# Paired products in the attention's first and last steps, a re-ordered first stage and an earlier first v load in an adaLN transformer block

## The chip, the cores and the metric

The kernel runs on one core of a Trainium2 chip. The metric is device time in microseconds (us) of one execution, as the median of several runs. The core has five engines that run their own instruction queues: TensorE (PE in the profile; its weight loads are PEld), VectorE (DVE), ScalarE (ACT), GpSimd (POOL) and SyncE (SP), which here issues the DMA transfers.

## The reference

One sequence of S = 2048 rows with D = 512 columns passes through an attention block of 32 heads (16 columns each) and a token-mixing MLP; both are modulated by six vectors that come from a condition `c`.

```python
mod = (silu(c) @ w_mod).reshape(1, 6, 1, 512)          # sa, ca, ga, sb, cb, gb
h = layernorm(x) * (1 + ca) + sa
q, k, v = split(h @ wqkv)                               # 32 heads of 16
o = softmax(q @ k.T * 16 ** -0.5) @ v
x = x + ga * (o @ wo)
h = layernorm(x) * (1 + cb) + sb
# B: token mixing by shifted columns, then an MLP 512 -> 1792 -> 512
t = gelu(layernorm(h) @ w1);  t = concat(four quarters of t, shifted by +1, -1, +2, -2 rows)
h1 = h + t @ w2
x = x + gb * (h1 + gelu(layernorm(h1) @ w3) @ w4)
```

All arithmetic is to float32 precision. The kernel gets it from split operands: a float32 matrix is held as a high part (rounded) and a low part (the rest), and a product is three matmuls (high by high, high by low, low by high).

## The kernel before, in words

**The work.** Rows come in four chunks of 512 (`NC`, index `ci`), four tiles of 128 rows each. Heads come in 16 pairs. An attention unit is one chunk of queries with one pair of heads: 64 units, each of 16 key tiles, so 1024 steps (`NS`), index `s`. A unit needs, before its exponentials, the row maximum of its scores. So each step has two parts: the score part of step `s`, and the maximum part of step `s + LEAD` with LEAD = 24.

- `score_part` (L1028): for head `j` of the pair, a matmul of 64 contraction rows with 512 columns (L1042) into a PSUM bank, then an exponential by ScalarE (L1038). The result is held as a 32-bit pattern whose upper half is the high part of the probability.
- `p_low` (L1078): the lower half becomes a float16 by a halving (L1093), on GpSimd for both heads at once, or on ScalarE in two halves (L1088) when the plan has GpSimd behind; the second ScalarE half waits in the list `second`.
- `pv_part` (L1100): probabilities by v, for the high parts (L1119) and the low parts of two steps (L1116), summed over a unit in one bank.
- `max_part` (L1010): another 64-row matmul (L1026) into a bank, and VectorE's `reduce_max` over it (L1022). When a unit's maxima are complete, `max_fin` (L1059) puts their negatives into rows of the query tile by eight small DMAs.

**Pairs.** Head 0 uses contraction rows 0 to 63 and head 1 rows 64 to 127. `row_pair(s, j)` (L1044) puts the score product of head `j` and the maximum product of head `1 - j` next to each other, on the two halves of the array. A counter `x` walks over 2 x 1024 such rows plus 48 ahead: `s, i = divmod(x, 2)`. For `s < 0` (24 steps) there are only maxima, for the last 24 steps only scores; there a row holds one product.

**The first stage** (to about 63 us in the profile). `x` is loaded by chunk. `ln1` (L536) takes statistics on VectorE (L372, L373), the reciprocal root on GpSimd (L376, L377), and normalizes each tile on VectorE (`apply`, L550) or ScalarE (`apply_act`, L553, the tiles in `LNA[ci]`). `mod_cols` (L567) computes sa and ca as rows (L572), copies them out of PSUM (L578, L580), turns them into columns by eight products with a 1x1 tile `one` (L587), and copies them to `modcol` (L591). `ln1_T` (L608) transposes each chunk in four slices of 128 columns (L618) and modulates them: for slices in `LNV[ci]` ScalarE makes the high part from PSUM (L627) and VectorE the whole (L630), for others ScalarE makes the whole (L623) and then the high part (L644); the low part is a subtraction (L636) on GpSimd for slices in `LNG[ci]`, else on VectorE. `qk_first` (L647) computes the first group's k for each chunk and q for chunk 0, 12 matmuls each (L361, L363, L365), and `qk_store` sends them to DRAM, from where `load_first` (L935) fetches the operands of the first unit. `v_weights` (L800) bounds |v| (L812 to L831), scales and splits v's weights. `v_tiles` (L754) computes v per 128 rows; `store` (L776) writes a tile to DRAM (`Vs`) and, once the attention's tiles exist (`direct`), also straight to its place in `vst`. The tiles stored before that are fetched from `Vs` by `before(s)` (L1590) at `s = -1` (the first entry of `VAT`, L1603).

**The order of work.** The order on every engine is written by a planner when the kernel is built: `Sched` keeps a clock per engine (P, A, D, G, and S for SP) and adds planned costs in nanoseconds. A `chain` is a sequence of operations on A, D and G with planned costs, a priority `prio` (lower goes first when an engine is behind) and a time at which it is ready. Generators (`mod_cols`, `ln1_T`, `qk_first`, the qkv groups, the tails) are the fillers on TensorE: each `yield` is one matmul's cost or a condition that must hold before it goes on. The main loop (L1666 to L1732) chooses at each point between a row, a block of pv columns (`do_cols`) and fillers. `one` is the planned time at which enough of the seven shared PSUM banks (`NSM`) are free; `need` (L1682) is how many products the row has. A row is entered when the time to it is under `STAY` (within a burst of up to `GRP` = 3 rows) or `BACK` (a new burst), where the next engine in need may be let run dry only to within `EARLY`; fillers may run past that time by `GRACE`. `budget(s)` spreads the fillers over the steps. `Sched.dma` plans SP: at least 475 ns per transfer.

**The last stage.** The tail of chunk `ci` (L1256: wo, LayerNorms, shifts, MLP) is filler during the attention of the next chunk; that of the last chunk runs after the attention.

Of the kernel before, what the change touches and what calls it, by code (L numbers as in the profile page):

```python
# [41 lines left out]
LAG = 2  # L42
CARRY = 3000.0
# [7 lines left out]
OVER = 3000.0  # L51
# [26 lines left out]
LNA = ((2, 3),) * 4  # L78
LNG = ((0, 1, 2),) * 4
LNV = ((1, 3),) * 4  # L80
# [11 lines left out]
GRACE = 400.0  # L92
PTLOW = 3
OVER = 1500.0

class Sched:
# [23 lines left out]
    def dma(self, start, o, i):  # L120

        n = 2 if o.dtype == BF16 else 4
        for d in o.shape:
            n *= d
        start(o, i)  # L125
        self.T["S"] = max(self.T["S"], self.T["P"]) + max(n / DBW, 475.0)
        return self.T["S"] + DLAT
# [205 lines left out]
def kernel(ctx, tc, A_x, A_wqkv, A_wo, B_w1, B_w2, B_w3, B_w4, c, w_mod, out):  # L333
# [57 lines left out]
    one = con.tile([1, 1], F32, name="one")  # L391
    pool.memset(one, 1.0)
# [143 lines left out]
    def ln1(ci):  # L536
        x = xt[ci]
        st, mv, rs = [sp.tile([P, TPC, n], F32, name=f"{nm}{ci}") for nm, n in (("st", 6), ("mv", 2), ("rs", 2))]
        left = [TPC]

        def stats(t):
            ln_stats(st[:, t, :], mv[:, t, :], x[:, t, :])

        def rstd():
            rstd_of(rs[:, :, 0], mv[:, :, 1])
            pool.tensor_tensor(rs[:, :, 1], mv[:, :, 0], rs[:, :, 0], op=OP.mult)
            pool.tensor_tensor(rs[:, :, 1], rs[:, :, 1], mone, op=OP.mult)

        def apply(t):
            dve.tensor_scalar(x[:, t, :], x[:, t, :], mv[:, t, 0:1], rs[:, t, 0:1], op0=OP.subtract, op1=OP.mult)  # L550

        def apply_act(t):
            act.activation(x[:, t, :], x[:, t, :], AF.Identity, bias=rs[:, t, 1:2], scale=rs[:, t, 0:1])  # L553
# [12 lines left out]

    def mod_cols():  # L567
# [18 lines left out]
        for i in range(8):  # L586
            te.matmul(b[:, i:i + 1], row[:, i * P:(i + 1) * P], one, start=True, stop=True, skip_group_check=True)  # L587
# [5 lines left out]
        sch.chain(("D", 120, cols), mark(("mod", 0)), mark(("mod", 1)), prio=0, bank=b)  # L593
# [14 lines left out]
    def ln1_T():  # L608
        yield lambda: ("mod", 0) in done and ("mod", 1) in done
        for ci in range(NC):  # L610
            x = xt[ci]
            left = [KT]
            for k in range(KT):
# [3 lines left out]
                for t in range(TPC):  # L617
                    te.transpose(b[:, t * P:(t + 1) * P], x[:, t, k * P:(k + 1) * P], ident)  # L618
                    yield 110
# [19 lines left out]
                def one(left=left, ci=ci):  # L639
# [3 lines left out]
                ops = (("A", 660, high), ("D", cD(), whole)) if k in LNV[ci] else (  # L643
                    ("A", 660, modulate), ("A", cA(), lambda f=f, hi=hi: act.activation(hi, f, AF.Copy)))  # L644
                sch.chain(*ops, (e, cG() if e == "G" else cD(), low), (None, 0, one))
# [154 lines left out]
    def v_weights(a):  # L800
# [4 lines left out]
        for i in range(2):  # L805
# [6 lines left out]
            sch.chain(("D", 1200, lambda x=f.bitcast(F32), t=t: dve.scalar_tensor_tensor(  # L812
# [13 lines left out]
        def cols():  # L826
            for i in range(2):
                dve.tensor_tensor_reduce(out=scr, in0=vb[:, i * P:(i + 1) * P], in1=ident, scale=1.0, scalar=0.0,
                                         op0=OP.mult, op1=OP.add, accum_out=vcol[:, 2 * a + i:2 * a + i + 1])
            dve.tensor_scalar(vcol[:, 2 * a:2 * a + 2], vcol[:, 2 * a:2 * a + 2], VHI, None, op0=OP.mult)  # L830
            dve.reciprocal(vb, vb)  # L831
            qfree.extend(ts)

        def scaled():
            for i, (f, f3) in enumerate(st):
                c = slice(512 * i, 512 * i + 512)
                sch.chain(("G", cG(), lambda f3=f3: pool.tensor_tensor(f3, f3, vb[:, None, :].to_broadcast([P, 2, 256]),
# [3 lines left out]
        sch.chain(("D", cD(256), bound), ("D", 1000, cols), (None, 0, scaled), bank=b)  # L841
# [202 lines left out]
    def row_pair(s, j):  # L1044

        parts = []
        if 0 <= s < NS:
            parts.append((j, score_part(s, j)))
        if s + LEAD < NS:
            parts.append((1 - j, max_part(s + LEAD, 1 - j)))  # L1050
        parts = [x for _, x in sorted(parts, key=lambda x: x[0])]
# [5 lines left out]
        return [partial(x[2], e) for x in parts]  # L1057
# [532 lines left out]
    def before(s):  # L1590
# [4 lines left out]
        if asked:  # L1595
# [23 lines left out]
    def one_row(x):  # L1619
# [3 lines left out]
        if second:  # L1623
            second.pop(0)()
# [22 lines left out]
    def do_cols(n):  # L1647
        sch.to("c")
# [17 lines left out]
    while x < end or pvs or acs:  # L1666
# [109 lines left out]
```

## Time and profile before

| | |
|---|---|
| median of 3 runs | 1995.44 us (1993.75 to 1995.77) |
| the profiled execution | 1993.19 us |
| its span, first to last instruction | 1991.4 us |
| mean granted TensorE clock | 0.991 |
| TensorE, VectorE, ScalarE, GpSimd busy | 1933.8, 1669.9, 1483.2, 1671.0 us |
| first maximum product (L1026) starts | 63.3 us |
| first score product (L1042) starts | 97.5 us |
| last maximum product | 1791.2 us |
| last score product | 1821.8 us |
| products of maxima, of scores | 2048, 2048 |

The views of the profile: the page with busy times, the chain of work that ended last and the costliest groups; windows (busy time of each engine in a stretch); groups by line; timelines (instructions in order of time, merged, with the idle time ahead of them and what ended it in brackets); and waits (engine and line that waited, for whom, total us, times, longest). Times are microseconds from the span's start, means of groups nanoseconds. Matmuls are pipelined: a matmul's duration is longer than the distance to the next one, so the price of a matmul is read from starts.

### The profile page before, as it was taken

The numbers are of one execution on the slowest core, as the hardware profiler recorded it, in microseconds if no ns is written. First come the engines' busy times: TensorE is split into PE (matmuls) and PEld (weight loads), VectorE is DVE, ScalarE is ACT, GpSimd is POOL, SyncE is SP. The second block draws the span as 40 slices with busy tenths as digits, with TensorE's granted clock in tenths as the row PEclk, the third lists the DMA queues.
The fourth block names the chain that finished last, engine by engine and source line by source line (L and its number), as shares of the span: only waits on it lengthen the run. The fifth ranks groups of instructions, "written<-read, shape, count | busy, mean of one in ns | idle before, by whom it ended". The sixth has DMA issues, their size and how long they took to land.

```text
span 1991.4 us, 42269 instructions
## 1 busy us (share of the span) xinstructions
PE 1933.8 (97%) x14480; PEld 1137.1 (57%) x14480; DVE 1669.9 (84%) x3010; ACT 1483.2 (74%) x3081; POOL 1671.0 (84%) x1601
## 2 busy tenths in 40 slices
PE   6989999999999999999999999999999999999899
PEld 4654565555445555555455555555555555555798
DVE  6969878899999888998999988888998888892643
ACT  5366888788878777787888877787888777786443
POOL 5368999999999998998898999888898988897532
PEclk8999999999999999999999999999999999999999
DMA  5675788786533433434433333344433334433432
GB/s 180 193 209 177 217 254 249 252 271 206 163 103 115 136 109 112 145 127 132 133 114 111 108 112 101 110 140 132 157 115 103 96 112 136 132 100 108 186 143 91
DMA packets 233082, 293.23 MB, mean 147 GB/s; under 512 B 125876, under 2 KB 178052, under 8 KB 216580
## 3 DMA queue, kind: packets, MB, share of 16 engines
q1 hardware_dynamic: 232868, 290.53, 45.8%
q8 instruction: 115, 1.88, 0.4%
q14 instruction: 99, 0.81, 0.1%
HBM read 225.81 MB, written 62.91 MB: 145 GB/s over the span
## 4 chain that ended last, share of the span: by engine, by line
PE 69%; DVE 9%; POOL 6%; ACT 6%; DMA 2%; issue 2%; SPq 1%; POOLq 0%; ACTq 0%; DVEq 0%
PE mb L1026 14%; PE sc L1042 11%; PE pv L1119 10%; PE w L361 7%; PE w L363 7%; PE w L365 7%; PE pv L1116 6%; DVE mx L1022 6%; POOL pt L1093 4%; ACT pt L1038 3%; PE ot L1151 1%; SPq L125 1%; DMA wr<-Ws 1%; PE q L365 1%; PE q L361 1%
## 5 line engine op out<-in xcount | busy, mean ns | idle before, releaser
L1022 DVE TENSOR_REDUCE mx<-mb 128x1 f32<-128x512 f32 x2048 | 1283.7, 682 | 117.2 <-PE mb L1026 88.6
L1093 POOL TENSOR_SCALAR pt<-pt 128x1024 f16<-128x1024 uint16 x980 | 1301.2, 1369 | 82.1 <-ACT pt L1038 78.6
L1038 ACT ACTIVATE pt<-sc 128x512 int32<-128x512 f32 x2048 | 1102.1, 602 | 272.5 <-PE mb L1026 181.2
L1026 PE MATMUL mb<-kst,qtl 64*128 64x512 f32 x2048 | 754.0, 455 | 18.3 <-DVE mx L1022 7.0
L1042 PE MATMUL sc<-qtl,kst 64*128 64x512 f32 x2048 | 728.3, 445 | 1.6 <-ACT pt L1038 0.7
L1026 PEld LDWEIGHTS mb<-kst,qtl 64*128 64x128 f32 x2048 | 347.1, 192 | 228.6 <-DVE mx L1022 108.4
L1042 PEld LDWEIGHTS sc<-qtl,kst 64*128 64x128 f32 x2048 | 334.9, 185 | 155.9 <-issue 52.5
L1119 PE MATMUL pv<-pt,vst 128*32 128x512 f16 x4096 | 348.8, 392 | 5.5 <-DMA vst<-Vs 4.9
L1116 PE MATMUL pv<-pt,vst 128*17 128x512 f16 (+1 forms) x2048 | 215.7, 397 | 4.6 <-POOL pt L1093 4.3
L1453 POOL TENSOR_TENSOR g<-xs,g 128x256 fp32r<-128x256 f32 (+2 forms) x144 | 103.4, 719 | 92.7 <-ACT g L1452 88.7
L1119 PEld LDWEIGHTS <-vst 128*32 128x32 bf16 x4096 | 112.3, 94 | 112.3 <-issue 48.1
L361 PE MATMUL w<-A,wr 128*128 128x256 f32 (+2 forms) x576 | 172.0, 299 | 0.6 <-ACT A L355 0.3
L363 PE MATMUL w<-A,wr 128*128 128x256 f32 (+2 forms) x576 | 170.0, 295 | 0.5 <-DVE A L351 0.3
L365 PE MATMUL w<-A,wr 128*128 128x256 f32 (+2 forms) x576 | 169.2, 294 | 0.0
L1116 PEld LDWEIGHTS <-vst 128*17 128x17 f16 (+1 forms) x2048 | 56.0, 90 | 130.5 <-issue 113.2
L361 PE MATMUL w<-wr,g 128*128 128x512 f32 x288 | 119.9, 416 | 0.8 <-ACT g L1452 0.6
L361 PEld LDWEIGHTS w<-A,wr 128*128 128x128 f32 x576 | 109.5, 190 | 18.0 <-issue 11.3
L365 PE MATMUL w<-wr,g 128*128 128x512 f32 x288 | 118.1, 410 | 0.2 <-POOL g L1453 0.2
L363 PEld LDWEIGHTS w<-A,wr 128*128 128x128 f32 x576 | 109.5, 190 | 14.4 <-issue 13.0
L363 PE MATMUL w<-wr,g 128*128 128x512 f32 x288 | 117.5, 408 | 0.0
L365 PEld LDWEIGHTS w<-A,wr 128*128 128x128 f32 x576 | 109.4, 190 | 12.9 <-issue 12.9
L1449 ACT ACTIVATE sq<-w 128x256 f32<-128x256 f32 (+2 forms) x144 | 55.8, 388 | 66.8 <-PE w L365 65.3
(150 smaller groups left out, 2095.6 us busy)
## 6 DMA issues: line engine op xcount, KB each, us to landing
wr<-Ws SPq DMA_DIRECT2D x80, 1024.0 KB
kst<-Ks SPq DMA_DIRECT2D x189, 256.0 KB
vst<-Vs SPq DMA_DIRECT2D x252, 192.0 KB
qtl<-Qs SPq DMA_DIRECT2D x192, 64.0 KB
Vs<-vt SPq DMA_DIRECT2D x32, 384.0 KB
Ws<-wq SPq DMA_DIRECT2D x40, 256.0 KB
Ws<-wst SPq DMA_DIRECT2D x40, 256.0 KB
wst<-in_B_w_dram SPq DMA_DIRECT2D x36, 256.0 KB
```

What stands on the lines that cost most here:

```text
L361: te.matmul(o, lh, rh, start=first, stop=False)
L363: te.matmul(o, lh, rl, start=False, stop=False)
L365: te.matmul(o, ll, rh, start=False, stop=last)
L1022: end = sch.crit("D", 605, e + PX, lambda: dve.reduce_max(mxs[u][:, j, g, c:c + 1], b, axis=AX.X))
L1026: return ready, lambda: te.matmul(b, lhs, kst[u % 3][r, c * CH:(c + 1) * CH], start=True, stop=True), after
L1038: ea = sch.crit("A", 480, e + PX, lambda: act.activation(pt[s][:, j], b, AF.Exp))
L1042: return ready, lambda: te.matmul(b, kst[u % 3][r, kt * P:(kt + 1) * P], qst[u][r], start=True, stop=True), after
L1093: e_low[s] = XP["G"] + sch.crit("G", 1345, ready, lambda: pool.tensor_scalar(o, i, 0.5, 1.0, op0=OP.mult, op1=OP.mult))
L1116: te.matmul(acc[r:r + n, :], v[:, (kt + i) % 4, c - n:c].bitcast(F16), pt[s + i].bitcast(F16)[:, j, 0::2], start=False, stop=kt == NKT - 2 ...
L1119: te.matmul(acc[r:r + 32, :], v[:, kt % 4, r:r + 32], pt[s].bitcast(F16)[:, j, 1::2], start=kt == 0, stop=False, skip_group_check=True)
L1449: sch.chain(("A", cA(n), lambda: act.activation(sq, b, AF.Square, scale=2.0)), ("D", cD(n), cube), ("A", cA(n), lambda: act.activation(sq, ...
L1453: ("G", cG(n), lambda: pool.tensor_tensor(lo, xs, hi, op=OP.subtract)), (None, 0, end), bank=b)
```

## The change

- **Paired rows** (`row_pair`, `width`, `one_row`, the loop): for `s < 0` one row holds the maximum products of both heads, for the last 24 steps one row holds the score products of both heads. Such a row advances `x` by two. A row always needs two banks; ahead of the attention it asks for `RES0` = 2 free ones beyond that, as before.
- **Waiting halves**: `do_cols` issues all halves in `second` before a block that has low parts; a double row takes up to two of them.
- **First stage, order**: priorities by chunk for statistics (`PST`), applies (`PAP`) and modulations (`PTR`) in place of 0, 0, 2, 2 for the LayerNorm and 1 for the modulation; planned costs nearer to the trace's; `ln1_T` no longer waits until the modulation columns are done.
- **First stage, engines**: new `LNA`, `LNG`, `LNV`.
- **Transposed modulation**: the eight products with `one` become eight `transpose`s with a corner of the identity; ScalarE copies the columns.
- **v's bound**: the factor VHI goes into the reduction, and the multiply of L830 goes away.
- **First v**: ahead of step -1, `before(s)` fetches each of the first four v tiles into place as soon as its store is done.
- **Constants of the planner**: SP's minimum 475 to 600 ns (`DMIN`), GRACE 400 to 200, BACK 150 to 100, EARLY 300 to 200, PX 270 to 265. OVER and OWE keep the values in force (1500).

```diff
+RES0 = 2
+DMIN = 600.0
+PAP = (1,0,-1,-1)
+PST = (1,0,0,1)
+PTR = (-1,1,1,0)
+TRX = 140.0
+DAP = 1000.0
-LNA = ((2, 3),) * 4
-LNG = ((0, 1, 2),) * 4
-LNV = ((1, 3),) * 4
+LNA = ((1,2,3),(0,1,2,3),(3,),(3,))
+LNG = ((0,1),(0,1,2,3),(0,2),(0,2))
+LNV = ((),(),(1,2,3),(1,3))
-GRACE = 400.0
+GRACE = 200.0
+BACK = 100.0
+EARLY = 200.0
+PX = 265.0
...
-                sch.chain(("A", 660, partial(apply_act, t)) if t in LNA[ci] else ("D", 460, partial(apply, t)), (None, 0, one),
-                          prio=2 * (ci > 1), ready=sch.T["G"] + XX)
-        sch.chain(*[("D", 670, partial(stats, t)) for t in range(TPC)], ("G", 1300, rstd), (None, 0, applies),
-                  prio=2 * (ci > 1), ready=arr["x", ci])
+                sch.chain(("A", 750, partial(apply_act, t)) if t in LNA[ci] else ("D", DAP, partial(apply, t)), (None, 0, one),
+                          prio=PAP[ci], ready=sch.T["G"] + XX)
+        sch.chain(*[("D", 840, partial(stats, t)) for t in range(TPC)], ("G", 1900, rstd), (None, 0, applies),
+                  prio=PST[ci], ready=arr["x", ci])
...
-            te.matmul(b[:, i:i + 1], row[:, i * P:(i + 1) * P], one, start=True, stop=True, skip_group_check=True)
-            yield 100
+            te.transpose(b[:, i:i + 1], row[:, i * P:(i + 1) * P], ident[0:1, 0:1])
+            yield 220
...
-            dve.tensor_scalar(modcol, b, 0.0, None, op0=OP.add)
+            act.activation(modcol, b, AF.Copy)
...
     def ln1_T():
-        yield lambda: ("mod", 0) in done and ("mod", 1) in done
         for ci in range(NC):
...
-                sch.chain(*ops, (e, cG() if e == "G" else cD(), low), (None, 0, one))
+                sch.chain(*ops, (e, 1320 if e == "G" else 670, low), (None, 0, one), prio=PTR[ci])
...
-                dve.tensor_tensor_reduce(out=scr, in0=vb[:, i * P:(i + 1) * P], in1=ident, scale=1.0, scalar=0.0,
+                dve.tensor_tensor_reduce(out=scr, in0=vb[:, i * P:(i + 1) * P], in1=ident, scale=VHI, scalar=0.0,
                                          op0=OP.mult, op1=OP.add, accum_out=vcol[:, 2 * a + i:2 * a + i + 1])
-            dve.tensor_scalar(vcol[:, 2 * a:2 * a + 2], vcol[:, 2 * a:2 * a + 2], VHI, None, op0=OP.mult)
...
     def row_pair(s, j):
-        parts = []
-        if 0 <= s < NS:
-            parts.append((j, score_part(s, j)))
-        if s + LEAD < NS:
-            parts.append((1 - j, max_part(s + LEAD, 1 - j)))
-        parts = [x for _, x in sorted(parts, key=lambda x: x[0])]
+        if s < 0:
+            parts = [max_part(s + LEAD, i) for i in (1, 0)][::-1]
+        elif s + LEAD >= NS:
+            parts = [score_part(s, i) for i in range(2)]
+        else:
+            parts = [(j, score_part(s, j)), (1 - j, max_part(s + LEAD, 1 - j))]
+            parts = [x for _, x in sorted(parts, key=lambda x: x[0])]
...
+    def width(s):
+        return 1 if 0 <= s < NS - LEAD else 2
...
+        if s < VAT[0]:
+            for kt in range(4):
+                if kt not in near and ("vk", 0, kt) in done:
+                    near.add(kt)
+                    sch.dma(dma.dma_start, vst[0][:, kt % 4], Vs[0, :, kt])
...
     def do_cols(n):
+        while second and any(lo for _, lo in pvs[:n]):
+            second.pop(0)()
...
-            need = (s >= 0) + (s + LEAD < NS)
+            need = 2
...
-            one = free[need - 1 + 2 * (s < 0)]
+            one = free[need - 1 + RES0 * (s < 0)]
...
-            x += 1
-            sch.credit = max(min(sch.credit + budget(s) / 2, CTOP), -OWE)
+            x += width(s)
+            sch.credit = max(min(sch.credit + budget(s) / 2 * width(s), CTOP), -OWE)
```

The planned costs inside `ln1_T`'s chains (660 to 760 and 770, 427 and 570 and the like) and those of `v_weights` change with it.

More of the change, by code (lines that the diff above doesn't have):

```diff
@@ L50 @@
 DEBT = 3000.0
-OVER = 3000.0
+OVER = 1500.0
 CROW, CCOL, CIN, CMID, COUT = 232.0, 230.0, 105.0, 95.0, 95.0
@@ L91 @@
 STAY = 200.0
-GRACE = 400.0
+GRACE = 200.0
 PTLOW = 3
-OVER = 1500.0
+BACK = 100.0
+EARLY = 200.0
+OWE = 1500.0
+PX = 265.0
 class Sched:
@@ L125, in dma @@
         start(o, i)
-        self.T["S"] = max(self.T["S"], self.T["P"]) + max(n / DBW, 475.0)
+        self.T["S"] = max(self.T["S"], self.T["P"]) + max(n / DBW, DMIN)
         return self.T["S"] + DLAT
@@ L390 @@
     mone = con.tile([P, 4], F32, name="mone")
-    one = con.tile([1, 1], F32, name="one")
-    pool.memset(one, 1.0)
     dve.memset(mone, -1.0)
@@ L586, in mod_cols @@
         for i in range(8):
-            te.matmul(b[:, i:i + 1], row[:, i * P:(i + 1) * P], one, start=True, stop=True, skip_group_check=True)
-            yield 100
+            te.transpose(b[:, i:i + 1], row[:, i * P:(i + 1) * P], ident[0:1, 0:1])
+            yield 220
         def cols():
-            dve.tensor_scalar(modcol, b, 0.0, None, op0=OP.add)
+            act.activation(modcol, b, AF.Copy)
             sch.free(b)
-        sch.chain(("D", 120, cols), mark(("mod", 0)), mark(("mod", 1)), prio=0, bank=b)
+        sch.chain(("A", 220, cols), mark(("mod", 0)), mark(("mod", 1)), prio=0, bank=b)
     gcol = qp.tile([P, 8], F32, name="gcol")
@@ L642, in one @@
                         done.add(("hT", ci))
-                ops = (("A", 660, high), ("D", cD(), whole)) if k in LNV[ci] else (
-                    ("A", 660, modulate), ("A", cA(), lambda f=f, hi=hi: act.activation(hi, f, AF.Copy)))
-                sch.chain(*ops, (e, cG() if e == "G" else cD(), low), (None, 0, one))
+                ops = (("A", 760, high), ("D", 750, whole)) if k in LNV[ci] else (
+                    ("A", 770, modulate), ("A", 570, lambda f=f, hi=hi: act.activation(hi, f, AF.Copy)))
+                sch.chain(*ops, (e, 1320 if e == "G" else 670, low), (None, 0, one), prio=PTR[ci])
     def qk_first(hi, lo):
@@ L811, in v_weights @@
             ab.append(t)
-            sch.chain(("D", 1200, lambda x=f.bitcast(F32), t=t: dve.scalar_tensor_tensor(
+            sch.chain(("D", 680, lambda x=f.bitcast(F32), t=t: dve.scalar_tensor_tensor(
                 t, x, -1.0, x, op0=OP.mult, op1=OP.max)), mark(keys[i]), ready=e)
@@ L836, in scaled @@
                 c = slice(512 * i, 512 * i + 512)
-                sch.chain(("G", cG(), lambda f3=f3: pool.tensor_tensor(f3, f3, vb[:, None, :].to_broadcast([P, 2, 256]),
+                sch.chain(("G", 1500, lambda f3=f3: pool.tensor_tensor(f3, f3, vb[:, None, :].to_broadcast([P, 2, 256]),
                                                                        op=OP.mult)),
@@ L840, in scaled @@
             done.add(("vcol", a))
-        sch.chain(("D", cD(256), bound), ("D", 1000, cols), (None, 0, scaled), bank=b)
+        sch.chain(("D", cD(256), bound), ("D", 1900, cols), (None, 0, scaled), bank=b)
         yield lambda: keys[2] in done and keys[3] in done
@@ L1056, in row_pair @@
         e = sch.put("P", CROW, max(x[0] for x in parts), mms)
-        return [partial(x[2], e) for x in parts]
+        return [partial(x[2], e) for x in (parts[::-1] if s < 0 else parts)]
+    def width(s):
+        return 1 if 0 <= s < NS - LEAD else 2
     def max_fin(u):
@@ L1622, in one_row @@
             fn()
-        if second:
-            second.pop(0)()
+        for _ in range(width(s)):
+            if second:
+                second.pop(0)()
     def col_at(y):
@@ L1647, in do_cols @@
     def do_cols(n):
+        while second and any(lo for _, lo in pvs[:n]):
+            second.pop(0)()
         sch.to("c")
```

2 lines of the change are left out of this document (1 added, 1 removed).

## The prediction

> **What bounds the kernel now.** I read the page first (busy shares, then the chain that ended last), then a table of windows cut at the stage borders, then the timelines of the first 103 us and of the last 30 us of the attention.
>
> ```profile
> span 1991.4 us, 42269 instructions
> PE 1933.8 (97%) x14480; PEld 1137.1 (57%) x14480; DVE 1669.9 (84%) x3010; ACT 1483.2 (74%) x3081; POOL 1671.0 (84%) x1601
> PE 69%; DVE 9%; POOL 6%; ACT 6%; DMA 2%; issue 2%; SPq 1%; POOLq 0%; ACTq 0%; DVEq 0%
> ```
>
> TensorE is the bound of the whole: 97% busy, 69% of the chain. But the change acts at the two ends, where the limits differ, so the windows count. Columns: window, its length, then busy time (instructions) of PE, weight loads, VectorE, ScalarE, GpSimd, then granted clock, DMA share, GB/s.
>
> ```profile
> 0.00:63.30 63.30, 46.29 (x200) 32.87 (x200) 44.73 (x83) 31.87 (x52) 35.87 (x52) 0.89 0.54 188
> 63.30:97.40 34.10, 32.92 (x166) 22.61 (x167) 32.66 (x59) 10.17 (x28) 8.67 (x12) 0.95 0.67 179
> 97.40:102.30 4.90, 2.06 (x8) 0.90 (x6) 3.61 (x7) 1.79 (x3) 1.98 (x2) 1.00 0.96 286
> ...
> 500.00:1000.00 500.00, 491.53 (x3920) 269.31 (x3916) 453.64 (x823) 401.21 (x840) 454.35 (x429) 1.00 0.41 129
> ...
> 1791.00:1822.00 31.00, 30.40 (x223) 14.19 (x221) 4.65 (x10) 25.56 (x52) 30.88 (x28) 1.00 0.09 21
> 1822.00:1991.40 169.40, 159.80 (x912) 138.80 (x911) 83.62 (x175) 65.93 (x150) 67.31 (x98) 0.99 0.41 151
> ```
>
> Before 63.3 us (LayerNorm, transposes, first k and q) TensorE has 17 us of gaps: a latency stage, and whatever it loses moves everything behind it. From 63.3 to 97.4 us (maxima only) VectorE works 32.66 of 34.10 us, so it binds there together with TensorE. From 97.4 to 102.3 us TensorE idles. In the mixed stage (500 to 1000 us stands for it) TensorE binds and VectorE and GpSimd have 9% to spare. From 1791 to 1822 us (scores only) GpSimd binds: 30.88 of 31.00 us. The last window is TensorE's again, with 9.6 us of gaps.
>
> **First stage.** These timeline rows (start, duration, engine, line) are its landmarks; below them stand three windows of VectorE alone, and the groups that give the prices (count, busy us, mean ns).
>
> ```profile
> 17.64 3.57 PE L587 MATMUL mc<-one,wm 1*128 1x1 f32 x16 [2.65 <-ACT wm L580]
> 56.12 0.39 PE L365 MATMUL k<-hT,wp 128*128 128x512 f32 x1
> 63.34 0.98 PE L1026 MATMUL mb<-kst,qtl 64*128 64x512 f32 x6 [1.35 <-DVE vr L773]
> 14.43 1.00 DVE L550 TENSOR_SCALAR xt<-xt,mv,rs 128x512 f32<-128x512 f32 x2 [1.50 <-POOL rs L377]
> 25.69 2.72 DVE L550 TENSOR_SCALAR xt<-xt,mv,rs 128x512 f32<-128x512 f32 x2
> 32.27 0.66 DVE L636 TENSOR_TENSOR hT<-h,hT 128x512 fp32r<-128x512 f32 x1
> 50.62 1.14 DVE L830 TENSOR_SCALAR vcol<-vcol 128x2 f32<-128x2 f32 x1
> 54.08 1.26 DVE L636 TENSOR_TENSOR hT<-h,hT 128x512 fp32r<-128x512 f32 x1
> 24.00:40.00 16.00, 15.72 (x27) 0.82 0.01 2
> 40.00:50.00 10.00, 8.20 (x14) 0.93 0.44 164
> 50.00:63.30 13.30, 10.05 (x14) 1.00 0.64 218
> L550 DVE TENSOR_SCALAR xt<-xt,mv,rs 128x512 f32<-128x512 f32 x8 | 8.7, 1131 | 1.5 <-POOL rs L377 1.5
> L630 DVE TENSOR_SCALAR h<-tr,modcol 128x512 f32<-128x512 f32 x8 | 6.3, 788 | 0.5 <-ACT hT L627 0.5
> L636 DVE TENSOR_TENSOR hT<-h,hT 128x512 fp32r<-128x512 f32 x4 | 3.3, 821 | 0.1
> L636 POOL TENSOR_TENSOR hT<-h,hT 128x512 fp32r<-128x512 f32 x12 | 16.1, 1358 | 3.1 <-ACT hT L644 1.4 <-ACT h L623 1.4 <-DVE h L630 0.3
> L623 ACT ACTIVATE h<-tr,modcol 128x512 f32<-128x512 f32 x8 | 6.2, 776 | 10.2 <-DVE gcol L601 4.7 <-PE tr L618 4.0 <-DVE hT L636 1.5
> L627 ACT ACTIVATE hT<-tr,modcol 128x512 fp32r<-128x512 f32 x8 | 6.1, 762 | 0.0
> L644 ACT ACTIVATE hT<-h 128x512 fp32r<-128x512 f32 x8 | 5.0, 631 | 0.3
> L553 ACT ACTIVATE xt<-xt,rs 128x512 f32<-128x512 f32 x8 | 6.0, 801 | 0.3 <-POOL rs L547 0.3
> ```
>
> The low part of chunk 0's last k-slice is made only at 32.27 us and that of chunk 3's at 54.08 us, both by VectorE, whose queue had other chunks' statistics or v's bound ahead of it; the last k matmul follows at 56.12 us. So VectorE's amount and order set the stage's end. The new tuples, counted over the four chunks: VectorE applies 7 tiles instead of 8 (-1.1 us), does 5 whole modulations instead of 8 (-2.4), 6 lows instead of 4 (+1.6), loses the small multiply of line 830 (-1.1, or nothing if what it waited for then delays the reciprocal behind it) and the copy of the modulation columns to ScalarE (-0.2): -3.2 us, at least -2.1. ScalarE gains one apply (+0.8) and three slices of 776 + 631 instead of 762 (+1.9); it was busy 31.87 of 63.3 us and can carry that. GpSimd loses two lows (-2.7).
>
> Three edits change order. The modulation columns become 8 one-pass transposes: 16 pieces took 3.57 us, so 8 at the same 0.22 us take 1.8, which is 1.8 us off the path to the first modulated slice. The x transposes no longer wait for the modulation. And chunk 0's slices go ahead of the statistics of chunk 3, which have fallen behind. The windows of VectorE say what order can bring: from 24 to 63.3 us it idled 0.3 + 1.8 + 3.2 = 5.3 us, in waits for its turn. I take 3.8 of them, so that amount and order give 3.2 + 3.8 = 7 us on the end of the k matmuls. The bounds are 3 (the amount alone) and 10 (all 5.3 us, and the 1.8 of the transposed columns kept). In exchange v's weights lose their place: if they come later, TensorE waits at 56 us where it now computes the first v tiles, and the lower end of 3 holds. The two SP constants (600 instead of 475 ns per transfer) only make the order plan for later arrivals.
>
> The page "SBUF — State Buffer", section "SBUF: two separate sides", of the Trainium skill says that VectorE and GpSimd share a port pair under an exclusive lock, so that the later one is blocked whole. The trace agrees: line 550's two tiles took 1.00 us at 14.43 us and 2.72 us at 25.69 us beside GpSimd's work. By that rule line 830's 1.14 us is a wait that moves to the next instruction, and the amount would be -2.1 instead of -3.2 us.
>
> **First v.** The first v tiles are stored before their place in the attention exists, and are fetched together at step -1:
>
> ```profile
> 98.91 2.00 SPq L125 DMA_DIRECT2D vst<-Vs  x2
> 102.32 0.41 PE L1119 MATMUL pv<-pt,vst 128*32 128x512 f16 x4 [2.67 <-DMA vst<-Vs]
> ```
>
> Fetched as soon as they are stored, while the maxima run, they are there in time. The two issues (1 us each) go to the SP queue that feeds the keys of the same stage, and hold nothing up for longer than that. The 2.67 us go; the products behind are ready, for scores ran up to the stall. What is next late is VectorE, which still has its maxima to finish: I take -2.7 us, bounds 0 and -2.7.
>
> **Paired products.** The mixed stage already shows the price of a pair, the score stage that of a single one (a block runs from its first row to the row behind it):
>
> ```profile
> 1005.08 0.50 PE L1026 MATMUL mb<-kst,qtl 64*128 64x512 f32 x1
> 1005.08 0.73 PE L1042 MATMUL sc<-qtl,kst 64*128 64x512 f32 x2
> 1005.42 0.62 PE L1026 MATMUL mb<-kst,qtl 64*128 64x512 f32 x2
> 1005.66 0.39 PE L1042 MATMUL sc<-qtl,kst 64*128 64x512 f32 x1
> 1005.98 0.50 PE L363 MATMUL wo<-wr,A 128*128 128x512 f32 x1
> ...
> 1796.66 0.73 PE L1042 MATMUL sc<-qtl,kst 64*128 64x512 f32 x3
> 1797.32 0.51 PE L365 MATMUL w<-wr,g 128*128 128x512 f32 x1
> ```
>
> Six products in three pairs take 0.90 us, three single ones 0.66 us. So 48 products cost 16 x 0.66 = 10.6 us single and 8 x 0.90 = 7.2 us paired: 3.4 us of TensorE saved at each end, and a little more for the block borders, about 4. Neither end is TensorE's alone. In the maxima stage VectorE must still reduce 48 tiles:
>
> ```profile
> 88.64 5.46 DVE L1022 TENSOR_REDUCE mx<-mb 128x1 f32<-128x512 f32 x9
> ...
> 1794.36 24.77 POOL L1093 TENSOR_SCALAR pt<-pt 128x1024 f16<-128x1024 uint16 x19
> ```
>
> At 5.46 / 9 = 0.61 us that is 29 us of its 34, with the v and k work on top. TensorE's free time there can only take k and v matmuls in advance, worth something later because the mixed stage is TensorE's. I take 1.5 of the 4 us. In the score stage GpSimd's 24 halvings at 24.77 / 19 = 1.30 us are 31 us, as long as the stage; the freed time brings the third chunk's last MLP products forward, which now cover the fourth chunk's LayerNorm. 1.5 of 4 us again; both have the bounds 0 and -4. The flush of waiting halves before a column block costs nothing where GpSimd makes them all, as its 30.88 us say.
>
> **The planner's constants** (shorter grace, later entry into rows, 265 instead of 270) change where a row enters in all 1000 mixed steps.
>
> ```profile
> PEld mb L1026 <- DVE mx L1022: 106.4, 294, 1.9
> ```
>
> Weight loads of maxima wait 106.4 us, in 294 times, for VectorE to free a bank: rows often enter too early, and entering up to 0.1 us later would give that time to fillers, as would 0.1 us of it for each of 294, 29 us at the most; but much is hidden under the matmul in flight. In the other direction a late row lets VectorE run dry. I take 0, with -10 and +10.
>
> **The sum.** 7 + 2.7 + 1.5 + 1.5 = 12.7 us off the profiled execution's 1993.2 us (span 1991.4 and 1.8 around it): 1980.5. The median of the three runs, 1995.44, lies 2.2 us above that execution; with it 1982.7. I say 1982.
>
> **The rivals.** First, VectorE binds from 14 to 97 us throughout, and the stages only get what it loses. For it: 32.66 of 34.10 us in the maxima stage; against it: the 5.3 us that it idled before. The first score then moves by the 3.2 us and nothing else stays: 1992, no change within what can be told. The page "TensorEngine Tiling (Array Packing)", section "Performance Considerations", of the Trainium skill speaks for this one: row tiles speed the array up but not the emptying of PSUM. The rows of VectorE and GpSimd above agree.
>
> Second, slower: in the mixed stage the later entry costs. The plan starts rows in bursts of at least three, so 2000 rows have some 667 entries, each up to 0.1 us nearer to VectorE running dry: 67 us. VectorE has 46 us in 500 to spare, 0.15 us a step, which pays for most of it. If a third of it, 22 us, turns up as time of the step, the sum is 1982.7 + 22 = 2005. It turns slower from 17 us, that is when over a quarter isn't covered. Against it: the 106.4 us say that rows enter early now, not late.
>
> Third, a larger gain: all of the two 4 us, the full 10 us of the first stage and the 10 us of the constants: 1993.2 - 10 - 2.7 - 8 - 10 + 2.2 = 1965. Half way there, 1972, is what I hold likelier.
>
> That the early v fetch does nothing, because the first tiles go directly to their place anyway, is part of the first rival.
>
> **How the numbers follow.** Forecast 0.60 (1976 to 1989), no change 0.13, slower 0.09, larger gain 0.18. What can be told from no change is 0.2%, 4 us: below 1991.4 is faster. Forecast and larger gain give 0.78, and a little of the first rival lies below the line: 0.80; 0.12 within; 0.08 above. The range from 1967 to 1993 leaves out the slower cases and the end of the larger gain.
>
> **What would show it.** Right: the last first-group k matmul at about 49 us, the first maximum at 56 to 58, no wait for v at the first pv, matmuls of maxima and scores in simultaneous twos at both ends, VectorE still full between the first maximum and the first score, about 34 us apart, GpSimd full over 31 us at the end. Wrong: a first score later than 93 us means that VectorE kept the stage; mixed steps over 1.71 us, where 1.69 is now (97.4 to 1791 us for 1000 steps), mean the second rival; a mixed stage shorter by over 10 us means that the constants carried the result.

## The result and the profile after

The changed kernel takes 1980.43 us (median of 4 runs, 1979.15 to 1981.5) against 1994.6 us of the kernel before (median of 4, 1993.4 to 1995.77): the ratio is 0.9929, with a 95% interval from 0.9912 to 0.9946, so 14.2 us faster. The changed kernel's executions also had a slightly higher granted TensorE clock; the last section works out that about 11.8 us are left at a like clock. The profiled execution took 1979.15 us. The page of the changed kernel begins:

```profile
span 1977.4 us, 42253 instructions
PE 1924.6 (97%) x14472; PEld 1126.1 (57%) x14472; DVE 1663.7 (84%) x3005; ACT 1490.4 (75%) x3106; POOL 1655.9 (84%) x1588
PE 73%; DVE 14%; ACT 4%; POOL 3%; DMA 3%; issue 2%; SPq 1%; POOLq 0%; ACTq 0%; DVEq 0%
```

TensorE still binds, and GpSimd's share of the chain has halved. Where the 14.0 us of span went is read from windows cut at the first maximum product, the first score product, the last maximum and the last score. First the last three stages of the kernel before, then all five of the changed one (columns as in the prediction: PE, PEld, DVE, ACT, POOL):

```profile
97.50:1791.20 1693.70, 1664.48 (x12984) 928.54 (x12981) 1504.32 (x2685) 1349.84 (x2801) 1528.34 (x1417) 1.00 0.47 147
1791.20:1821.80 30.60, 30.00 (x222) 14.03 (x221) 4.45 (x10) 25.16 (x52) 30.48 (x27) 1.00 0.09 21
1821.80:1991.40 169.60, 160.00 (x913) 138.96 (x912) 83.62 (x175) 66.13 (x151) 67.51 (x98) 0.99 0.41 151
```

```profile
0.00:58.30 58.30, 41.30 (x194) 26.39 (x194) 41.65 (x79) 33.57 (x58) 33.52 (x48) 0.97 0.58 203
58.30:90.80 32.50, 29.66 (x169) 20.65 (x169) 31.51 (x57) 10.73 (x30) 9.77 (x12) 1.00 0.77 198
90.80:1774.90 1684.10, 1661.30 (x12946) 920.66 (x12945) 1499.01 (x2679) 1346.72 (x2803) 1516.61 (x1406) 1.00 0.47 146
1774.90:1807.90 33.00, 32.69 (x261) 19.28 (x261) 7.54 (x17) 30.72 (x64) 29.16 (x27) 1.00 0.27 89
1807.90:1977.40 169.50, 159.65 (x911) 139.13 (x909) 83.97 (x175) 68.70 (x154) 66.86 (x97) 0.98 0.41 150
```

The first stage is 5.0 us shorter, the maxima stage 1.7 (34.2 to 32.5), the mixed stage 9.6, the score stage 2.4 us longer, the tail the same. The counts of matmuls tell what the mixed stage lost: 38 of them (12984 to 12946), and the score stage gained 39 (222 to 261). Fillers have moved from the one to the other, as far as they fit beside the paired scores.

In the first stage these rows answer to those of the prediction:

```profile
16.23 0.65 PE L596 MATMUL mc<-ident,wm 1*128 1x1 f32 x8 [2.33 <-ACT wm L589]
18.01 0.15 ACT L600 ACTIVATE modcol<-mc 128x8 f32<-128x8 f32 x1
25.60 0.66 DVE L644 TENSOR_TENSOR hT<-h,hT 128x512 fp32r<-128x512 f32 x1
39.70 1.75 DVE L838 RECIPROCAL vb<-vb 128x256 f32<-128x256 f32 x1
42.23 0.63 PE L626 MATMUL tr<-ident,xt 128*128 128x128 f32 x4 [1.48 <-DVE h L638]
48.63 1.69 DVE L471 TENSOR_TENSOR wp<-wst,wp 128x512 fp32r<-128x512 f32 x1
50.24 0.68 DVE L644 TENSOR_TENSOR hT<-h,hT 128x512 fp32r<-128x512 f32 x1
50.98 0.50 PE L374 MATMUL k<-hT,wp 128*128 128x512 f32 x1 [1.38 <-DVE hT L644]
51.68 0.69 DVE L644 TENSOR_TENSOR hT<-h,hT 128x512 fp32r<-128x512 f32 x1
52.77 0.40 PE L376 MATMUL k<-hT,wp 128*128 128x512 f32 x1
58.27 0.97 PE L1033 MATMUL mb<-kst,qtl 64*128 64x512 f32 x6 [1.34 <-DVE vr L781]
L559 DVE TENSOR_SCALAR xt<-xt,mv,rs 128x512 f32<-128x512 f32 x7 | 5.9, 881 | 0.0
L644 DVE TENSOR_TENSOR hT<-h,hT 128x512 fp32r<-128x512 f32 x6 | 5.4, 901 | 0.1
L638 DVE TENSOR_SCALAR h<-tr,modcol 128x512 f32<-128x512 f32 x5 | 3.8, 782 | 0.0
```

The modulation columns take 0.65 us instead of 3.57, though not at the same granted clock (1.00 here, 0.50 there; see the last section). Chunk 0's last low is made at 25.60 us instead of 32.27. But chunk 3's last low comes at 51.68 us (54.08 before), and the last k matmul starts at 52.77 (56.12): half of the early lead of 6.7 us is lost again. The middle rows show where. v's bound, which ends with the reciprocal, now stands ahead of chunk 2's slices on VectorE (its last step ended at 53.42 us before, ahead of chunk 3's last slice, and ends at 41.45 us now), and TensorE waits for the slice behind it at 42.23 us. At 50.98 us TensorE waits for a low part that VectorE makes behind the low part of v's weights (L471).

### The profile page after: what moved, and what is told of

Its sections match the earlier page's. It is cut to its first block, busy times and chain, and to the rows that moved or that the text cites. A ratio compares the mean times of both kernels' runs of the same rounds, so it can differ in the third digit from the quotient of the medians.

```text
span 1977.4 us, 42253 instructions
## 1 busy us (share of the span) xinstructions
PE 1924.6 (97%) x14472; PEld 1126.1 (57%) x14472; DVE 1663.7 (84%) x3005; ACT 1490.4 (75%) x3106; POOL 1655.9 (84%) x1588
## 4 chain that ended last, share of the span: by engine, by line
PE 73%; DVE 14%; ACT 4%; POOL 3%; DMA 3%; issue 2%; SPq 1%; POOLq 0%; ACTq 0%; DVEq 0%
PE mb L1033 15%; PE sc L1049 11%; PE pv L1130 10%; DVE mx L1029 8%; PE w L372 7%; PE w L376 7%; PE w L374 7%; PE pv L1127 6%; ACT pt L1045 2%; POOL pt L1104 1%; SPq L136 1%; PE ot L1162 1%; PE xT L1240 1%; DVE tst L383 1%; PE mr L674 1%
## 5 line engine op out<-in xcount | busy, mean ns | idle before, releaser
L1033 PEld LDWEIGHTS mb<-kst,qtl 64*128 64x128 f32 x2048 | 346.5, 192 | 231.0 <-DVE mx L1029 117.1
L1130 PE MATMUL pv<-pt,vst 128*32 128x512 f16 x4096 | 353.7, 393 | 1.7 <-DMA vst<-Vs 1.4
L1127 PEld LDWEIGHTS <-vst 128*25 128x25 f16 (+1 forms) x2048 | 55.5, 90 | 134.0 <-issue 117.6
L376 PE MATMUL w<-wr,g 128*128 128x512 f32 x288 | 117.1, 407 | 0.2 <-POOL g L1464 0.2
```

The lines of the kernel that those rows point to most:

```text
L376: te.matmul(o, ll, rh, start=False, stop=last)
L1033: return ready, lambda: te.matmul(b, lhs, kst[u % 3][r, c * CH:(c + 1) * CH], start=True, stop=True), after
L1127: te.matmul(acc[r:r + n, :], v[:, (kt + i) % 4, c - n:c].bitcast(F16), pt[s + i].bitcast(F16)[:, j, 0::2], start=False, stop=kt == NKT - 2 ...
L1130: te.matmul(acc[r:r + 32, :], v[:, kt % 4, r:r + 32], pt[s].bitcast(F16)[:, j, 1::2], start=kt == 0, stop=False, skip_group_check=True)
```

## The experiments

The change falls into four parts: P, the paired rows with all that belongs to them in the loop (the flush of waiting halves too, which can act in the mixed steps); V, the early fetch of the first v tiles; C, the constants GRACE, BACK, EARLY and PX; F, the first stage with DMIN. Four kernels leave one part out of the changed kernel, four add one part to the kernel before, two split P, and two are controls. All compute the whole reference. Theory A is the forecast's: each part has its worth, and the worths add. The rivals are B (the mixed stage's length is a matter of how a plan falls), C (the v stall only moves VectorE's idle time) and D (the constants carry the gain).

### One part left out

Without P the branches for `s < 0` and for the last steps go, and a row is one product there again:

```diff
-        if s < 0:
-            parts = [max_part(s + LEAD, i) for i in (1, 0)][::-1]
-        elif s + LEAD >= NS:
-            parts = [score_part(s, i) for i in range(2)]
...
-            need = 2
+            need = (s >= 0) + (s + LEAD < NS)
...
-            x += width(s)
+            x += 1
```

> The changed kernel with single products in the steps with only maxima or only scores, all else kept. Theory A (each part has its own worth, and the worths add): the maxima stage is 34 us again instead of 32.5, the score stage loses 4 us of TensorE time, and the time rises by 3 to 5 us over the changed kernel's, to 1983.5 to 1985.5. Theory B (the mixed stage's length is a matter of how the plan happens to fall, and a part's worth is smaller than that): the two end stages change as in A, but the mixed stage moves by several us either way, and the time lies anywhere from 1976 to 1988.

Measured: 1997.31 us, ratio to the kernel before 1.0011 (1.0001 to 1.0022). All of the gain is gone, four times what theory A gives. The stages of the table below say where: maxima stage 33.4 us, and a tail of 184.7 us, with 968 matmuls instead of 911, which the mixed stage had left over without being shorter for it.

```profile
93.10:1780.40 1687.30, 1660.44 (x12898) 918.68 (x12895) 1493.02 (x2669) 1346.82 (x2790) 1518.41 (x1404) 0.99 0.47 146
...
1814.10:1998.80 184.70, 172.91 (x968) 150.79 (x965) 87.98 (x183) 70.10 (x159) 68.88 (x100) 0.98 0.40 147
```

Without V:

```diff
-        if s < VAT[0]:
-            for kt in range(4):
-                if kt not in near and ("vk", 0, kt) in done:
-                    near.add(kt)
-                    sch.dma(dma.dma_start, vst[0][:, kt % 4], Vs[0, :, kt])
```

> The changed kernel, with the first v tiles fetched together at step -1 as before. Theory A: TensorE waits for v again at the first pv, 2.5 us, and the time is 2.5 us more, 1983. Theory C (VectorE binds until well behind the first pv, so the stall only moves its idle time): a wait of 2.5 us is seen at the first pv, but the time rises by under 1 us.

Measured: 1982.29 us, ratio 0.9937 (0.992 to 0.9954). It is 1.9 us over the changed kernel's median, with overlapping intervals. Neither theory had the place right: TensorE's first pv matmul does not wait for v, and the weight load ahead of it only for 0.25 us.

```profile
93.19 1.71 SPq L136 DMA_DIRECT2D vst<-Vs  x2
...
96.55 0.41 PE L1130 MATMUL pv<-pt,vst 128*32 128x512 f16 x4
```

The changed kernel's plan has other matmuls between the first score (92.4 us) and the first pv, so that even the late fetch lands in time. VectorE, ScalarE and GpSimd run the same instructions in the same order as in the changed kernel, so this pair shows V alone: 1.9 us by the medians, and about 0.6 when both are brought to a like clock by the line of the last section.

Without C:

```diff
-GRACE = 200.0
+GRACE = 400.0
...
-BACK = 100.0
-EARLY = 200.0
-PX = 265.0
```

> The changed kernel with the planner's constants of before (grace 400, back 150, early 300, PX 270). Theory A with the constants at nothing, as forecast: 1980 within 1 us, steps of the mixed stage the same. Theory D (the constants carry what the mixed stage gained, which is 6 to 7 us from the first score to the last maximum beyond the v wait): 1986 to 1987.

Measured: 1986.61 us, ratio 0.9958 (0.9943 to 0.9973). That is the time that theory D gives, but not its place: of the 4.5 us that the rest is longer than the changed kernel's (table below), the mixed stage has 2.5, the score stage 3.2, and the tail is 1.2 us shorter.

Without F the tuples, priorities, planned costs, the columns by matmul with `one` and the multiply of L830 come back:

```diff
-LNA = ((1,2,3),(0,1,2,3),(3,),(3,))
-LNG = ((0,1),(0,1,2,3),(0,2),(0,2))
-LNV = ((),(),(1,2,3),(1,3))
+LNA = ((2, 3),) * 4
+LNG = ((0, 1, 2),) * 4
+LNV = ((1, 3),) * 4
...
-            te.transpose(b[:, i:i + 1], row[:, i * P:(i + 1) * P], ident[0:1, 0:1])
+            te.matmul(b[:, i:i + 1], row[:, i * P:(i + 1) * P], one, start=True, stop=True, skip_group_check=True)
```

> The changed kernel with the first stage of before (order, engines, modulation columns, planned costs, SP's minimum). Theory A: first maximum at 63.3 us instead of 58.3, everything behind it later by the same 5 us: 1985.5. Theory B: first maximum at 63.3 us, but the sum off from that by several us through the mixed stage.

Measured: 1988.49 us, ratio 0.997 (0.996 to 0.998). The first maximum is at 61.6 us, 3.3 later and not 5 as both theories say; but the mixed stage is 11.0 us longer. The four parts, by leaving out, would be worth 17 + 2 + 6 + 8 = 33 us, of a gain of 14.

### One part added to the kernel before

The edits are those of the diff above, one part at a time.

> The kernel before with paired products at both ends alone. Theory A: 1994.6 less 3 to 5, so 1990 to 1991.5, with the maxima stage shorter by 1.7 us. Theory B: the end stages as in A, the sum anywhere within some us of that.

Measured: 1992.34 us, ratio 0.9988 (0.9978 to 0.9997), a gain of 2.4 us (0.6 to 4.4). The maxima stage is 32.7 us instead of 34.2, nearly as in theory A. The 2.4 us may be no gain at all: these ten executions had a mean granted clock of 0.993, the 31 of the kernel before beside them 0.990, and the line of the last section gives 3 us for that.

> The kernel before with only the early fetch of the first v tiles. Theory A: no wait for v at the first pv, 1994.6 less 2.5: 1992. Theory C: no wait for v, but the time within 1 us of 1994.6.

Measured: 1990.98 us, ratio 0.9975 (0.9962 to 0.9989), a gain of 5 us (2.2 to 7.6). In this plan the wait was there, and it is gone: 2.1 us from the first score (95.78 us) to the first pv, instead of 4.8 us. The order on VectorE, ScalarE and GpSimd is that of the kernel before throughout, so this gain is V's; at a like clock it is 4.0 us.

```profile
97.86 0.41 PE L1126 MATMUL pv<-pt,vst 128*32 128x512 f16 x4
```

> The kernel before with only the four constants of the planner changed (grace 200, back 100, early 200, PX 265). Forecast: 1994.6 within 1 us. Theory D: 1988, with the mixed stage shorter by 6 us. The second rival of the prediction: slower, 2005.

Measured: 2000.39 us, ratio 1.0023 (1.0011 to 1.0035). The same constants that seemed to give 6 us cost 4.6 here. Theory D falls, and so does the forecast's "within 1 us".

> The kernel before with only the first stage changed (order, engines, modulation columns, planned costs, SP's minimum). Theory A: first maximum at 58.3 us and 1994.6 less 5: 1989.6. Theory B: first maximum at 58.3 us, the sum off from that by several us.

Measured: 1996.44 us, ratio 1.0006 (0.9995 to 1.0017). The first maximum comes at 58.4 us, 4.9 earlier, and nothing is left of it at the end: the tail is 7.7 us longer. By adding, the four parts give 2.4 + 5 - 4.6 - 1.2 = 1.6 us, of a gain of 14; brought to a like clock, they give a loss of 5 us, of a gain of 11.8. Theory A falls.

### The controls: one nanosecond

What does a new plan do by itself? PX is a number of the planner's reckoning. One nanosecond of it has no meaning for the chip, but it orders the instructions anew:

```diff
-PX = 265.0
+PX = 266.0
```

> The changed kernel with PX 266 instead of 265 ns: nothing is changed but the planner's reckoning, by one nanosecond. Theory A (the stages' worths are those of the parts): within 1 us of the changed kernel's 1980. Theory B: off from it by 3 to 15 us, in the mixed stage and the tail, with the first stage and the maxima stage as in the changed kernel.

Measured: 1988.96 us, ratio 0.9959 (0.9944 to 0.9974): 8.5 us over the changed kernel by the medians, 6.0 by the ratios.

```diff
-PX, XX = 270.0, 170.0
+PX, XX = 271.0, 170.0
```

> The kernel before with PX 271 instead of 270 ns, nothing else. Theory A: within 1 us of the kernel before. Theory B: off from it by 3 to 10 us either way.

Measured: 2009.46 us, ratio 1.006 (1.004 to 1.0081): 12 us over the kernel before. The mixed stages of the two controls:

```profile
92.60:1789.40 1696.80, 1668.11 (x12984) 927.86 (x12982) 1501.08 (x2687) 1345.09 (x2803) 1526.29 (x1415) 0.99 0.47 146
```

```profile
98.00:1806.50 1708.50, 1672.02 (x12972) 932.15 (x12971) 1503.69 (x2684) 1349.54 (x2801) 1524.09 (x1413) 0.99 0.47 145
```

The second does the work of the kernel before (12972 matmuls against 12984) in 14.8 us more; TensorE's gaps are 36.5 us against 29.2, the rest is within its busy time. Not all of it is the plan: both controls had a lower granted clock in their profiled executions than the kernels that they came from (0.988 against 0.994, 0.986 against 0.991). With all runs brought to a clock of 0.991 by the line of the last section, the first control lies about 5 us over the changed kernel and the second 11 us over the kernel before; whether the new order itself lowers the clock is not shown. In the first control, one place holds most of the 5 us, TensorE's wait for a later fetch of v, here in the control and in the changed kernel:

```profile
555.43 1.04 PE L1130 MATMUL pv<-pt,vst 128*32 128x512 f16 x8 [5.30 <-DMA vst<-Vs]
```

```profile
549.32 0.63 PE L1130 MATMUL pv<-pt,vst 128*32 128x512 f16 x8 [1.42 <-DMA vst<-Vs]
```

So theory B holds, with one control for each kernel: a difference of some 5 to 10 us between two plans says nothing by itself of the part that was edited.

### P in two halves

Where an edit touches only late steps, the plan ahead of it stays the same, and the rest can be compared. Pairs in the maxima steps only:

```diff
-            parts = [score_part(s, i) for i in range(2)]
+            parts = [score_part(s, j)]
...
-        return 1 if 0 <= s < NS - LEAD else 2
+        return 2 if s < 0 else 1
...
-            need = 2
+            need = 1 + (s + LEAD < NS)
```

> The changed kernel with pairs in the maxima steps only; the score steps have single products again. Theory A (the pairs at the end are worth what they free of TensorE in the score stage, about 4 us): no more than about 40 filler matmuls fit into the score stage instead of 79, the rest stands after it, and the time is 3 to 5 us more than the changed kernel's, 1984. Theory B (one plan differs from another by several us, whatever the cause): 1980 to 1997, with the mixed stage or the tail off by more than the score stage can explain.

Measured: 1988.29 us, ratio 0.9956 (0.994 to 0.9973), so 5.4 us (by the ratios) to 7.9 us (by the medians) over the changed kernel, and 6 to 7 at a like clock. Theory A gave 3 to 5. The mixed stage is the changed kernel's (1685.1 us, the same 12946 matmuls, and the same order on the other engines up to 1777 us). Then:

```profile
1775.90:1808.90 33.00, 32.13 (x236) 15.68 (x234) 6.46 (x15) 28.68 (x61) 32.02 (x29) 1.00 0.26 85
1808.90:1985.10 176.20, 166.23 (x935) 144.42 (x934) 85.81 (x177) 67.59 (x152) 67.96 (x98) 0.98 0.39 145
```

The score stage takes the same 33.0 us but holds 25 matmuls fewer (236 against 261), and the tail holds 24 more (935 against 911) and is 6.7 us longer, 0.28 us for each. The 25 are all products that read a gelu's result (`g` in the trace: 47 in the stage with pairs, 22 without). That is the worth of pairs at the end: the stage takes as long without them, TensorE being over 97% busy in it either way, and what TensorE does less of in it, the tail has to do in full.

Pairs in the score steps only:

```diff
-            parts = [max_part(s + LEAD, i) for i in (1, 0)][::-1]
+            parts = [max_part(s + LEAD, 1 - j)]
...
-        return 1 if 0 <= s < NS - LEAD else 2
+        return 2 if s + LEAD >= NS else 1
...
-            need = 2
+            need = 1 + (s >= 0)
```

> The changed kernel with pairs in the score steps only; the maxima steps have single products again. Theory A: the maxima stage is 34 us instead of 32.5 and the time 1.5 to 2 us more, 1982. Theory B: 1976 to 1997.

Measured: 1981.54 us, ratio 0.9923 (0.9908 to 0.9937): no difference from the changed kernel that the intervals show. The maxima stage is 33.1 us, 0.6 longer.

### All kernels, by stage

Microseconds of the profiled executions; "rest" is all from the first score on.

```
kernel      first stage  maxima   mixed  score   tail     rest
before          63.3      34.2   1693.7   30.6  169.6   1893.9
changed         58.3      32.5   1684.1   33.0  169.5   1886.6
a_noP           59.7      33.4   1687.3   33.7  184.7   1905.7
a_noV           59.4      33.0   1685.1   33.0  169.4   1887.5
a_noC           58.9      33.0   1686.6   36.2  168.3   1891.1
a_noF           61.6      32.6   1695.1   31.6  166.0   1892.7
a_px1           59.3      33.3   1696.8   31.5  167.3   1895.6
a_pairmax       57.9      32.9   1685.1   33.0  176.2   1894.3
a_pairsc        58.5      33.1   1677.2   35.4  174.7   1887.3
b_P             63.1      32.7   1690.3   33.8  170.7   1894.8
b_V             61.2      34.6   1693.1   30.5  170.5   1894.1
b_C             61.7      34.0   1699.2   34.3  170.1   1903.6
b_F             58.4      33.3   1691.5   33.5  177.3   1902.3
b_px1           63.0      35.0   1708.5   33.2  172.0   1913.7
```

Read down the columns, the parts show up in spite of the plans. F: the first stage is 57.9 to 59.7 us in the eight kernels with it (mean 58.8) and 61.2 to 63.3 in the six without (62.3): 3.5 us. Pairs of maxima: 32.5 to 33.3 us with, 33.1 to 35.0 without; by the means 0.3 us beside the new first stage and 1.8 beside the old. Pairs of scores: the rest is 1886.6 to 1895.6 us in six plans with them (mean 1891.4; a_noV repeats the changed kernel's plan and is left out) and 1893.9 to 1913.7 in six without (mean 1902.2; b_V left out likewise). The groups hardly overlap, and differ by 11 us. Both kernels of the case have the shortest rest of their group. The clock is in these means too: 0.986 (b_px1), 0.988 (a_px1), 0.990 (b_C, b_V), 0.991 (before, a_noV) and 0.992 to 0.994 in the others; by the line of the last section, about 1 of the 11 us is the clock.

## Why the prediction was right, and where it wasn't

The forecast was 1982 us and 12.7 us of gain; measured were 1980.43 and 14.2. The sum came out, but with luck: the first stage was over-sized, the pairs of scores were under-sized, and v's wait is not a term of the changed kernel at all. The same change with one nanosecond more in PX takes 1988.96 us, at the edge of the 1976 to 1989 us to which the forecast gave its chance.

**First stage: 7 us forecast, 5.0 in the two profiles, 3.5 as the mean over the kernels.** The amount came out: VectorE's busy time to the first maximum fell from 44.73 to 41.65 us, 3.1 against the 3.2 worked out. In part that is luck: the modulations are 2.5 us less, as worked out, but the applies 2.8 less instead of 1.1, the lows 2.1 more instead of 1.6, and the low parts of v's weights, which the working left out, 1.0 more. Line 830's 1.14 us did go: the reciprocal behind it takes 1.75 us, and took 1.74 before, so no wait moved on to it. The order was over-sized. The 7 us were to be seen at the end of the k matmuls, and 3.4 were (56.12 to 52.77 us); the 3.8 us taken for the order supposed that VectorE's waits were what could be won, while v's bound came to stand ahead of chunk 2's slices. The price of a modulation piece, 0.22 us, was one at half the clock: eight transposes took 0.65 us and not 1.8.

The working took no account of the clock, and it is a rival for part of this gain. Its mean before the first maximum was 0.89 in the kernel before and 0.97 in the changed one. Among kernels with a clock of 0.88 to 0.92, the first maximum comes at 58.9 to 59.4 us with the new first stage (a_noC, a_px1, a_noV) and at 61.2 to 63.3 with the old one (b_V, a_noF, b_C, before). At nearly the same clock that is 1.8 to 2.3 us (0.91 and 0.92) or 2.3 to 4.0 us (0.88 and 0.89).

**First v: 2.7 us forecast.** In the kernel before, the wait goes as forecast, and the gain alone is 2.2 to 7.6 us. In the changed kernel the term is not there: its plan hides the late fetch anyhow, and leaving V out costs 1.9 us at most. That the early fetch might do nothing was named as part of the first rival, but for another reason: without V the tiles are still fetched (at 93.19 us), only in time.

**Pairs of maxima: 1.5 us forecast, 1.7 us in the two profiles, less by themselves.** Beside the old first stage the pairs alone give 1.5 us (b_P), beside the new one 0.6 (a_pairsc) or 0.3 (by the means), and the time of a_pairsc cannot be told from the changed kernel's. VectorE binds there with 31.51 us of 32.50, as said. Its own work in the stage fell by 1.2 us (32.66 to 31.51, with 57 instructions instead of 59), which is most of the 1.7. That TensorE's fell from 32.92 to 29.66 us could add little, for VectorE takes one maximum after the other:

```profile
58.83 4.88 DVE L1029 TENSOR_REDUCE mx<-mb 128x1 f32<-128x512 f32 x8 [0.61 <-PE mb L1033]
```

**Pairs of scores: 1.5 us forecast with 4 as the bound; 5.4 to 7.9 us measured.** This is the term that was furthest off. The price of the pairs was right:

```profile
1795.66 0.96 PE L1049 MATMUL sc<-qtl,kst 64*128 64x512 f32 x6
1796.55 0.63 PE L1130 MATMUL pv<-pt,vst 128*32 128x512 f16 x8
```

Six products take 0.89 us. What failed is the step after it: "the freed time brings the third chunk's last MLP products forward, which now cover the fourth chunk's LayerNorm". The tail does not need them as cover; TensorE was 160 of 169.6 us busy in it, and 24 matmuls more made it 6.7 us longer. And GpSimd did not stay the bound: the plan gives ScalarE six halves of the halvings in the stage (none in the kernel before, two in a_pairmax), and GpSimd's busy time falls from 30.48 us of 30.6 to 29.16 of 33.0. Four of the six:

```profile
1789.80 2.68 ACT L157 ACTIVATE pt<-pt 128x512 f16<-128x512 uint16 x4
```

**The constants: 0 forecast, with 10 to either side.** That they have no sign of their own fits: 6 us of gain in one kernel and 4.6 us of loss in the other. The reason given does not show. Entering later was to cut the waits of weight loads for VectorE. They were 108.4 us in the kernel before and 117.1 in the changed one:

```profile
L1033 PEld LDWEIGHTS mb<-kst,qtl 64*128 64x128 f32 x2048 | 346.5, 192 | 231.0 <-DVE mx L1029 117.1
```

The constants alone did not cut them either: 108.4 to 114.3 us beside the kernel before (b_C), 111.6 (a_noC) to 117.1 beside the changed one. What the constants did cannot be told from what one nanosecond does, another plan. The bounds of 10 us that were put on them were the right size for a re-plan.

**The rivals.** The first (VectorE keeps the stage) fell for the stages together, though it holds from 58 to 91 us. The second (later entry costs) is not shown: b_C is slower, but so is b_px1, whose constants of entry are those of before. The changed kernel's mixed step is 1.684 us, under the 1.69 of before. The third (a larger gain) did not come; half way between 1965 and 1982 would be 1973.5, not 1972.

**The signs that were named.** The first score before 93 us, mixed steps under 1.71 us and no wait for v at the first pv came as said. The last first-group k matmul came at 52.77 us and not at 49, the first maximum at 58.3, just behind the 56 to 58, and GpSimd was not full at the end. The mixed stage is 9.6 us shorter, close to the 10 that were to mean that the constants carried the result; but in b_C the constants alone make that stage 5.5 us longer (1699.2 against 1693.7), and in the changed kernel the score stage took over 39 of its matmuls.

Open is what makes one plan 10 us better than another. Single waits are part of it, as the 5.30 us for v in a_px1. TensorE's gaps in the mixed stage do not rank the plans: 29.2 us in the kernel before, 36.5 in b_px1, but 25.5 in b_C, which is slower than the kernel before. Which decision of the planner brings the difference is not known. By the mean of the groups the change would be worth about 3.5 us of first stage, 1 of maxima and 11 of the rest, 15 to 16 us; that so much of it is due to the pairs of scores, of which the direct comparison shows 5.4 to 7.9, is not settled. For the two kernels of the case, the stages give 5.0 + 1.7 + 7.3 us (first, maxima, rest). With single scores at the end the changed kernel's rest is 1894.3 us, the kernel before's is 1893.9, so the pairs of scores can account for the 7.3; but v's wait and the new plan lie in the same stretch, and the runs do not part them.

## What to carry to other kernels

Where an order is planned by a simulation, a change of any cost re-orders everything behind it; a control that changes nothing but the plan (here one nanosecond) gives the spread, and only differences beyond it, or ones seen at a place where the plan is the same, belong to the edit. Time that an engine saves in one stage can be worth its full length, even if that stage gets no shorter, if a later stage is bound by that engine and work can be moved forward into the saved time. Count instructions by stage before and after: 38 out here and 39 in there explain more than the busy shares do.

## What the runs showed of the hardware

The granted clock of TensorE goes in steps: in windows of 3.4 us cut at its steps it reads 0.50 or 1.00 (in the kernel before 0.50 from 17.6 to 24.4 us, 1.00 to 27.8, 0.50 to 31.2). What that does to one group of instructions is seen at the modulation columns. The rows are windows over the 16 pieces of the kernel before, over the same 16 pieces in b_V, and over the 8 transposes of the changed kernel; the clock is the third number from the end:

```profile
17.64:21.21 3.57, 3.57 (x17) 3.56 (x18) 1.74 (x5) 0.00 (x0) 0.00 (x0) 0.50 1.05 383
17.14:19.08 1.94, 1.94 (x17) 1.93 (x18) 1.74 (x5) 0.00 (x0) 0.00 (x0) 1.00 1.05 389
16.23:16.88 0.65, 0.65 (x9) 0.64 (x10) 0.16 (x1) 0.65 (x2) 0.00 (x0) 1.00 1.03 381
```

The same 16 pieces take 3.57 us at 0.50 and 1.94 us at 1.00.

The time of one and the same program goes with the mean granted TensorE clock of the execution. Over 57 executions of the kernel before, the mean clock lay between 0.986 and 0.994, and a straight line through them falls by 1.0 us for 0.001 of clock: 1990.1 to 1990.9 us at 0.994, 1997.0 to 1999.4 us at 0.987; single executions scatter by over a microsecond about the line. The old first stage, whose order is the same in six kernels, began the first maximum at 61.2 to 63.3 us. So profiles that differ by less than some us should be compared at like clocks. The changed kernel's four runs (0.991 to 0.994) lie at 1982.2 us when brought to 0.991 by that line, the kernel before at 1994.0, which leaves 11.8 of the 14.2 us. The clock may in part be the change's own doing: before the first maximum it was 0.86 to 0.92 in the six kernels with the old first stage and 0.88 to 0.97 in the eight with the new. In the two main profiles TensorE's gaps in that stage are 17.0 us each; all of the 5.0 us lie in its busy time (46.29 to 41.30 us), and part of that is the clock (0.89 and 0.97).
